# A mixing and low-rank MLP kernel with the order of its first stage rewritten

## The chip, the cores and the metric

One core of a Trainium2 chip runs the whole program. The metric is the device time of one execution in microseconds (us). Five engines work side by side, each with its own queue of instructions that it takes in order: TensorE (PE, matrix products into PSUM), VectorE (DVE), ScalarE (ACT), GpSimd (POOL) and SyncE (SP, which here only issues DMAs). DMAs are issued by SP and by POOL.

## The reference

The input x is 8 x 3136 x 256 in float32. Each batch goes through a two-dimensional Fourier transform of which the real part is kept, then through a low-rank mixing along the sequence, then through a two-layer MLP along the channels, with two residual sums:

```
X = real(fft(fft(x, axis=1), axis=2))      # per batch: sequence, then channels
h = X.transpose(0, 2, 1) @ U @ V           # U: 3136 x 32, V: 32 x 3136
u = X + h.transpose(0, 2, 1)
out = u + maximum(u @ w_ch1, 0) @ w_ch2    # w_ch1: 256 x 1024, w_ch2: 1024 x 256
```

## The kernel before, in words

The sequence transform is a product with tables of sines (tabs, `tabs[0]`) and cosines (tabc, `tabs[1]`), which the kernel computes itself. Symmetries cut it down: a batch of x is loaded forwards (xf) and reversed (xr), in two halves a = 0, 1 of the sequence each; the sums and differences of both, along the sequence and along the channels, are what is multiplied. This is the *fold*: `along_d` (L247 to 251) and `alone` (L253) work along the channels into EOF_ and EOR_, `mirror` (L257) and `half` (L261) along the sequence into G, one G for each parity and for even and odd batches. The tables have eight rows of tiles i = 0 to 7. Rows i = 0, 2, 4, 6 come from `pho` and are called odd rows here, rows 7, 5, 3, 1 come from `phe` and are called even rows: of an even row only half is computed, and `mirror_even` (L234) copies the other half.

The first stage, which builds the tables and the rest, has an order written out by hand (`tc.manual_schedule()` up to `order.close()`): each engine takes its instructions in the order of the source. After it the Tile framework's scheduler orders the instructions itself, and a barrier for the scheduler alone (`tc.no_sync_barrier()`) separates the two. What the stage holds:

- `phase` (L155 to 159), two DVE operations, reduces an angle to a whole number of a turn; `sine` (L161) is one ACT operation, `cosine` (L167) two.
- `cosine_odd(i)` (L240) derives an odd row of the cosine table from the sine table by one ACT copy. `cosine_even` computes an even row from `phe` and mirrors it.
- `halve(t)` (L225, DVE) scales row 7 of table t.
- `fold_u` (L180, DVE, six operations) folds U, which is loaded forwards (UF: two indirect DMAs issued by POOL, L52) and reversed (UR), into GU.
- `transform_u(typ)` (L199) multiplies folded U with table typ and appends the result to the tables, so that the product of x with U comes out of the same matmuls as the transform. It is a generator of four steps: contract on PE with the odd rows (pk = 1), its evict on ACT, contract with the even rows (pk = 0), its evict. `us` and `uc` are its lists of steps for the sine and the cosine table: us[0] and uc[0] need only odd rows, us[2] and uc[2] only even rows.
- MSN, MC: small tables for the transform along the channels, from the phase `pd`.
- POOL clears G of odd batches, VA and TA (L442 to 449), and later issues the loads of the weights (L499 to 504), converts half of W1 (L507), and issues the gathers of xf for the next batch (`load_f`, L52). SP issues the loads of xr (`load_r`, L69) and of one odd row of both (`load_0`, L75 and 78). `load_x(b)` is all of these for a batch.
- Steps 8 and on of `transform(0)`: eight `seq` (L264: eight or four matmuls each into pt, L297; every second one has its result combined by DVE into A, B and tab), eight `chan` (the transform along the channels, L322 to 326, into S and T), `lowrank` (L329: TA, and one row of VA).

Then the main loop runs over 49 chunks of 512 rows: `front(c)` (L355) forms u with the matmul ph (L360) and two DVE sums (L368), `first_product` (L374, relu on ACT at L382), `second_product` (L385, matmuls at L396, sums by DVE at L402 to 405). The steps of `transform(b)` for the next batch, the fold first, are spread over the chunks by a list of due places (`due`).

The hand-written order in the middle of the first stage, before:

```
phases and sines of odd rows; phases, sines and mirrors of even rows
halve(0); fold_u(); POOL: memsets of G[1], VA, TA, iota of pint
cosine_odd x4; us[0]; us[1]; cosine_even(7); cosine_even(5); us[2]; us[3]
cosine_even(3); cosine_even(1); uc[0]
xr halves 0 and 1 along the channels (DVE; odd columns on POOL)
phase of pd; uc[1]; MSN, MC; halve(1); uc[2]; uc[3]
xf along the channels, mirror, half; POOL: weights; load_x(1); seq ...
```

Of the kernel before, what the change touches and what calls it, by code (L numbers as in the profile page):

```python
# [11 lines left out]
FP32 = mybir.dt.float32  # L12
# [7 lines left out]
NI = 8  # L20
NQ = 393
# [6 lines left out]
def kernel(  # L28
# [9 lines left out]
    nc = tc.nc  # L38
# [8 lines left out]
    cpool = ctx.enter_context(tc.tile_pool(name="cpool", bufs=1))  # L47
# [13 lines left out]
    xf = cpool.tile([KP, 2, NI, D], FP32, name="xf")  # L61
    xr = cpool.tile([KP, 2, NI, D], FP32, name="xr")

    def load_f(b, a):
        gather(xf[:PQ, a].rearrange("p i d -> p (i d)"), x, B * S // 8 - 1,
               xidx[:PQ, b, a:a + 1], 8 * D, D)

    def load_r(b, a):
        nc.sync.dma_start(out=xr[:PQ, a].rearrange("p i d -> p (i d)"), in_=rev(x, b, a, D))  # L69

    def load_0(t, dst_f, dst_r, b, w):


        lo = t.offset + b * S * w
        nc.sync.dma_start(out=dst_f[PQ:KP],  # L75
                          in_=bass.AP(t.tensor, lo + (NI - 1) * w,
                                      [[w, 1], [HALF * w, 2], [-w, NI], [1, w]]))
        nc.sync.dma_start(out=dst_r[PQ:KP].rearrange("p a i d -> p a (i d)"),
                          in_=bass.AP(t.tensor, lo, [[w, 1], [HALF * w, 2], [1, NI * w]]))

    def load_x(b):
        for a in range(2):
            load_f(b, a)
            load_r(b, a)
        load_0(x, xf, xr, b, D)

    order = ExitStack()
# [15 lines left out]
                      in_=bass.AP(moe_U.tensor, moe_U.offset + (S - 784) * R,  # L103
                                  [[8 * R, PQ], [-HALF * R, 2], [1, 8 * R]]))
# [17 lines left out]
    EOR_ = cpool.tile([KP, 2, NI, 258], BF16, name="eor")  # L122
# [9 lines left out]
    def const(v):  # L132
# [8 lines left out]
    tabs = [cpool.tile([KP, NI, 2, QW], BF16, name="tabs", tag="tabs"),  # L141
            cpool.tile([KP, NI, 2, QW], BF16, name="tabc", tag="tabc")]
# [18 lines left out]
    def sine(out_, y, bits, sgn):  # L161
        unit = TWO_PI / 2 ** bits
        pp = out_.shape[0]
        nc.scalar.activation(out_, y, AF.Sin, scale=-sgn * unit,
                             bias=(c_pi if sgn > 0 else c_npi)[:pp])

    def cosine(out_, y, bits):  # L167
        pp = y.shape[0]
        ab = gen.tile(list(y.shape), FP32, tag="ab", name="ab")
        nc.scalar.activation(ab[:], y, AF.Abs, bias=c_half[bits][:pp])  # L170
        nc.scalar.activation(out_, ab[:], AF.Sin, scale=TWO_PI / 2 ** bits, bias=c_nhp[:pp])  # L171

    NH = NQ // 2 + 1
    pho = gen.tile([KP, NI // 2, 2, NQ], I32, name="pho", bufs=1)
    phe = gen.tile([KP, NI // 2, 2, NH], I32, name="phe", bufs=1)
# [4 lines left out]
    def fold_u():  # L180
        nc.vector.tensor_tensor(uo[:], UF[:], UR[:, :, ::-1, :], op=AL.subtract)
        nc.vector.tensor_tensor(ue[:], UF[:], UR[:, :, ::-1, :], op=AL.add)
        for par in range(2):
            op = AL.add if par == 0 else AL.subtract
            nc.vector.tensor_tensor(GU[par][:, 0], uo[:, 0], uo[:, 1], op=op)  # L185
            nc.vector.tensor_tensor(GU[par][:, 1], ue[:, 0], ue[:, 1], op=op)
# [10 lines left out]
    def kp(i):  # L197
        return KP if i == NI - 1 else PQ
# [3 lines left out]
    def transform_u(typ):  # L202

        for pk in (1, 0):
            def contract(pk=pk):
                pu = PU[typ, pk] = psum.tile([P, NI, R], FP32, tag="dft", name="pu", bufs=3)
                for io in range(NI):
                    pn = (io + 1) % 2
                    m = kp(io)
                    j0 = NQ - 1 - (4 * 97 + (io + 1) // 2)  # L210
                    ks = ktiles(pk)
                    for n, i in enumerate(ks):
                        w = tabs[typ][:kp(i), i, pn, j0:j0 + 4 * (m - 1) + 1:4]
                        nc.tensor.matmul(pu[:m, io, :], w, GU[pn][:kp(i), typ, i, :],  # L214
                                         start=(n == 0), stop=(n == len(ks) - 1))

            def evict(pk=pk):
                pu = PU[typ, pk]
                nc.scalar.copy(tabs[typ][:PQ, 0:NI - 1, pk, NQ:QW], pu[:PQ, 0:NI - 1, :])
                nc.scalar.activation(tabs[typ][:, NI - 1, pk, NQ:QW], pu[:KP, NI - 1, :],  # L220
                                     AF.Copy, scale=hv[:KP])
            yield contract
            yield evict

    def halve(t):  # L225
        nc.vector.tensor_single_scalar(tabs[t][:, NI - 1, :, :NQ], tabs[t][:, NI - 1, :, :NQ],
                                       hv[:KP], op=AL.mult)
# [6 lines left out]
    def mirror_even(t, i):  # L234

        odd_m = (i + 1) // 2 % 2 == 1
        sgn = 1.0 if odd_m == (t == 0) else -1.0
        nc.scalar.activation(cells(t, i, 0, 1, NH - 1, 1), cells(t, i, NQ - 1, -1, NH - 1, 0),  # L238
                             AF.Copy, scale=sgn)

    def cosine_odd(i):

        nc.scalar.activation(cells(1, i, 1, 1, NQ - 1, 0), cells(0, i, NQ - 2, -1, NQ - 1, 1),
                             AF.Copy, scale=1.0 if i % 4 == 0 else -1.0)

    def along_d(a, src, dst, part):
        lo, hi = src[:, a, :, 1:128], src[:, a, :, 255:128:-1]  # L247
        if part == 0:
            nc.vector.tensor_tensor(dst[:, a, :, 1:128], lo, hi, op=AL.subtract)
        else:  # L250
            nc.vector.tensor_tensor(dst[:, a, :, 129:256], lo, hi, op=AL.add)  # L251

    def alone(a, src, dst):  # L253

        nc.gpsimd.tensor_copy(dst[:, a, :, 128:257:128], src[:, a, :, 0:129:128])  # L255
# [98 lines left out]
    def front(c):  # L354

        u = cp.tile([P, 2, CH], BF16, tag="u", name="u", bufs=2)
        for s in range(2):
            ph = psum.tile([P, CH], FP32, tag="dft", name="ph", bufs=3)
            for b, lo, hi, col in pieces(c):
                nc.tensor.matmul(ph[:, col:col + hi - lo], TA[b % 2][:, s * P:(s + 1) * P],  # L360
                                 VA[b % 2][:, lo:hi], start=True, stop=True)
            for b, lo, hi, col in pieces(c):
                d = ST[b]
                if lo <= HALF:
                    src = (d["S"] if s == 0 else d["T"])[:, lo:hi]
                else:
                    src = (d["T"] if s == 0 else d["S"])[:, S - lo:S - hi:-1]
                nc.vector.tensor_tensor(u[:, s, col:col + hi - lo], ph[:, col:col + hi - lo],  # L368
                                        src, op=AL.add)
        ut = cp.tile([P, 2 * CH // P, P], BF16, tag="ut", name="ut", bufs=3)  # L370
        nc.sync.dma_start_transpose(out=ut[:], in_=u.rearrange("p s r -> p (s r)"))
        CK[c] = dict(u=u, ut=ut)
# [59 lines left out]
    for m, i in enumerate(range(0, NI, 2)):  # L432
        phase(pho[:, m], krow[:KP], ncol[:KP, i:i + 1], 15)
        sine(tabs[0][:, i, :, :NQ], pho[:, m], 15, 1)
    for m, i in enumerate((7, 5, 3, 1)):
        phase(phe[:, m], krow[:KP, :, NH - 1:], ncol[:KP, i:i + 1], 15)
        sine(tabs[0][:, i, :, NH - 1:NQ], phe[:, m], 15, 1)
        mirror_even(0, i)
    halve(0)
    fold_u()  # L440
    for par in range(2):
        nc.gpsimd.memset(G[1][par][:, :, 258:GW].bitcast(I32), 0)  # L442
    for s in range(2):
# [3 lines left out]
        nc.gpsimd.memset(TA[s][R:R + 1, P:P + 1], -1.0)  # L447
    nc.gpsimd.iota(pint[:], pattern=[[0, 1]], base=D, channel_multiplier=-1)
    nc.gpsimd.memset(pint[0:1], P)
    us, uc = list(transform_u(0)), list(transform_u(1))  # L450
    for i in range(0, NI, 2):
        cosine_odd(i)
    us[0]()
    us[1]()

    def cosine_even(m, i):
        cosine(tabs[1][:, i, :, NH - 1:NQ], phe[:, m], 15)
        mirror_even(1, i)

    cosine_even(0, 7)  # L460
    cosine_even(1, 5)
    us[2]()
    us[3]()
    cosine_even(2, 3)
    cosine_even(3, 1)
    uc[0]()
    for a in range(2):
        for part in range(2):
            along_d(a, xr, EOR_, part)
        alone(a, xr, EOR_)  # L470
    nc.vector.memset(lrow[:, 1, 0:1], 128.0)
    nc.vector.tensor_single_scalar(pcol[:], pcol[:], 1.0 / D, op=AL.mult)
    pd = gen.tile([P, 2 * P], I32, name="pd", bufs=1)
    phase(pd[:], lrow.rearrange("p a l -> p (a l)"), pcol[:], 17)
    uc[1]()
    sine(MSN[:, 0:128], pd[:, 0:128], 17, -1)
    sine(MSN[:, 128:256], pd[:, 128:256], 17, 1)
    cosine(MC[:], pd[:], 17)
# [26 lines left out]
    nc.gpsimd.memset(msr[:, :, 0:1], 1.0)  # L505
    nc.gpsimd.memset(msr[:, :, 1:2], -1.0)
    nc.gpsimd.tensor_copy(W1[:, 1, :], w1t[:])  # L507
    load_x(1)
    for step in list(transform(0))[8:]:
        step()  # L510
    order.close()
    tc.no_sync_barrier()
    setup.close()
    cp = ctx.enter_context(tc.tile_pool(name="cp", bufs=2))
    front(0)

    due = {}
    for b in range(1, B):
# [47 lines left out]
```

## Time and profile before

| what | value |
|---|---|
| median of three runs | 503.09 us (502.71 to 503.56) |
| the profiled execution | 503.75 us in all, span 502.0 us |
| busy share of the span | PE 95%, DVE 62%, ACT 56%, POOL 11% |
| first matmul of U (L214) | 17.00 us after the span's start |
| first matmul of batch 0's transform (L297) | 31.06 us |
| first matmul of the first product (L380) | 50.56 us |
| DMA traffic | 67.13 MB, 134 GB/s on average |

The span runs from the first to the last instruction; the rest of an execution lies around it. In the timeline a line gives the start and the length in us, the engine, the source line, the operation, the tile written and those read, the shape, the number of merged instructions, and in brackets the idle time of the engine before it with what ended it. PE is shown busy while matmuls stand in its pipeline, so its share isn't its speed. The spans of POOL are rough.

### The profile page before, as it was taken

The page shows a single profiled execution, that of the slowest core. Times are in us where ns is not written, and L with a number is a line of the kernel's source. Part 1 is how long each engine was busy: PE and PEld are TensorE (multiplying, and loading weights), DVE is VectorE, ACT ScalarE, POOL GpSimd, SP SyncE. Part 2 cuts the span into 40 slices and gives each one's busy share as a digit, 9 for nine tenths or more (in the row PEclk, how much of TensorE's full clock was granted, in tenths as well). Part 3 has the DMA queues.
Part 4 walks back from the last instruction along what each step waited for, and adds up shares of the span by engine and source line. Part 5 has one row for each costly group of instructions (what it writes and reads, how often), then busy time and mean ns, then how long its engine had stood idle before and what let it go on. Part 6 is the DMA issues. An engine that isn't in the chain of part 4 may idle for free.

```text
span 502.0 us, 8180 instructions
## 1 busy us (share of the span) xinstructions
PE 476.3 (95%) x3152; PEld 305.7 (61%) x3152; DVE 312.0 (62%) x693; ACT 281.6 (56%) x537; POOL 56.3 (11%) x79
## 2 busy tenths in 40 slices
PE   0687999999999999999999999999999999999997
PEld 0653566666666666666666666666666666666665
DVE  9985999999989776963474345344343344344243
ACT  4844644665466544655456544655456544755652
POOL 8460212223141100200000000000000000000000
PEclk9999899999999999999999999999999999999999
DMA  6793797889969983333223332333224332333433
GB/s 187 193 200 108 133 254 206 190 232 255 215 183 239 294 208 88 97 92 114 64 63 85 106 84 60 109 80 110 63 64 85 105 85 63 100 89 107 125 85 126
DMA packets 83472, 67.13 MB, mean 134 GB/s; under 512 B 53467, under 2 KB 79905, under 8 KB 80281
## 3 DMA queue, kind: packets, MB, share of 16 engines
q1 hardware_dynamic: 79864, 51.86, 40.3%
q0 software_dynamic: 3568, 14.76, 11.1%
q8 instruction: 24, 0.39, 0.4%
q14 instruction: 16, 0.12, 0.1%
HBM read 29.26 MB, written 25.69 MB: 109 GB/s over the span
## 4 chain that ended last, share of the span: by engine, by line
PE 93%; DVE 4%; ACT 2%; issue 0%; DVEq 0%; ACTq 0%
PE p L396 34%; PE p L380 34%; PE pt L297 14%; PE ph L360 4%; PE pst L322 2%; PE pst L324 2%; PE pu L214 1%; DVE phe L157 1%; PE ptt L334 1%; DVE pho L159 1%; ACT tabc L171 1%; DVE phe L159 0%; DVE pho L157 0%; ACT tabc L238 0%; ACT ab L170 0%; ACT S L326 0%
## 5 line engine op out<-in xcount | busy, mean ns | idle before, releaser
L382 ACT ACTIVATE h<-p 128x512 bf16<-128x512 f32 x392 | 218.4, 597 | 148.7 <-PE p L380 148.4
L380 PE MATMUL p<-u,w 128*128 128x512 bf16 x784 | 210.3, 381 | 2.0 <-DVE u L368 1.7
L396 PE MATMUL p<-w,h 128*128 128x256 bf16 x1568 | 203.5, 273 | 0.0
L396 PEld LDWEIGHTS <-h 128*128 128x128 bf16 x1568 | 153.2, 98 | 59.0 <-DVE o L405 0.3
L380 PEld LDWEIGHTS <-w 128*128 128x128 bf16 x784 | 76.1, 98 | 65.4 <-issue 5.4
L402 DVE TENSOR_TENSOR o<-p,ut 128x4 f32<-128x4 f32 (+1 forms) x100 | 16.3, 163 | 137.6 <-PE p L396 136.5
L297 PE MATMUL pt<-tabc,g 98*128 98x425 bf16 (+1 forms) x256 | 57.5, 350 | 0.0
L297 PEld LDWEIGHTS <-g 98*128 98x128 bf16 (+1 forms) x384 | 38.3, 100 | 31.5 <-issue 4.4
L405 DVE TENSOR_TENSOR o<-p,ut 128x254 f32<-128x254 f32 (+1 forms) x100 | 40.7, 407 | 0.0
L404 DVE TENSOR_TENSOR o<-p,ut 128x254 f32<-128x254 f32 (+1 forms) x100 | 40.6, 406 | 0.0
L301 ACT COPY ev<-pt 128x425 f32<-128x425 f32 x32 | 16.5, 516 | 39.2 <-PE pt L297 30.6
L368 DVE TENSOR_TENSOR u<-ph,S 128x512 bf16<-128x512 f32 (+15 forms) x64 | 35.0, 556 | 0.8 <-PE ph L360 0.8
L368 DVE TENSOR_TENSOR u<-ph,T 128x512 bf16<-128x512 f32 (+15 forms) x64 | 34.9, 556 | 0.3 <-PE ph L360 0.3
L297 PE MATMUL pt<-tabs,g 98*128 98x425 bf16 (+1 forms) x128 | 30.3, 361 | 0.0
L360 PE MATMUL ph<-va,ta 128*128 128x512 bf16 (+18 forms) x128 | 29.8, 333 | 0.5 <-ACT ta L337 0.5
L52 POOL DMA_INDIRECT xf<-in_x_dram,xidx x16 | 21.5, 1344 | 53.6 <-DVE eof L251 25.2
L310 DVE TENSOR_TENSOR B<-pt,ev 128x393 bf16<-128x393 f32 (+1 forms) x16 | 9.3, 584 | 23.8 <-PE pt L297 23.8
L255 POOL CAST eof<-xf 99x16 bf16<-99x16 f32 x16 | 14.0, 877 | 84.6 <-DVE eos L258 52.9
L214 PE MATMUL pu<-gu,tabs 98*98 98x32 bf16 (+1 forms) x64 | 6.0, 251 | 17.0 <-DVE gu L185 17.0
L322 PE MATMUL pst<-A,mc 128*128 128x392 bf16 (+1 forms) x64 | 21.2, 331 | 0.7 <-DVE A L310 0.7
L258 DVE TENSOR_TENSOR eos<-eof,eor 99x1024 bf16<-99x1024 bf16 (+2 forms) x34 | 21.3, 659 | 0.2
L324 PE MATMUL pst<-B,msn 128*128 128x392 bf16 (+1 forms) x64 | 21.1, 330 | 0.0
(86 smaller groups left out, 290.8 us busy)
## 6 DMA issues: line engine op xcount, KB each, us to landing
out_dram<-o SPq DMA_DIRECT2D x48, 512.0 KB
xr<-in_x_dram SPq DMA_DIRECT2D x16, 784.0 KB
ut<-u SPq DMA_TRANSPOSE x49
w<-in_moe_w_ch_dram POOLq DMA_DIRECT2D x1, 512.0 KB
out_dram<-o SPq DMA_DIRECT2D x4, 128.0 KB
va<-in_moe_V_dram POOLq DMA_DIRECT2D x2, 196.0 KB, 6.4
xf<-in_x_dram,xidx POOLq DMA_INDIRECT x16, 8.6
w<-in_moe_w_ch_dram POOLq DMA_DIRECT2D x1, 256.0 KB, 5.8
```

Source lines behind the costliest of these rows:

```text
L52: nc.gpsimd.indirect_dma_start(out_, None, bass.AP(t.tensor, t.offset, [[w, rows], [1, w]]), bass.IndirectOffsetOnAxis(idx, 0), element_of ...
L258: nc.vector.tensor_tensor(EOS[:, a, :, cols], EOF_[:, a, :, cols], EOR_[:, a, ::-1][:, :, cols], op=op)
L297: nc.tensor.matmul(pt[:], g[:kp(i), i, col:col + P], tabs[t][:kp(i), i, par, :], start=(n == 0), stop=(n == len(mm) - 1))
L322: nc.tensor.matmul(pt[:, :hi - lo], MC[:, h * P:(h + 1) * P], d["A"][:, lo:hi], start=True, stop=False)
L324: nc.tensor.matmul(pt[:, :hi - lo], MSN[:, h * P:(h + 1) * P], d["B"][:, lo:hi], start=False, stop=True)
L360: nc.tensor.matmul(ph[:, col:col + hi - lo], TA[b % 2][:, s * P:(s + 1) * P], VA[b % 2][:, lo:hi], start=True, stop=True)
L368: nc.vector.tensor_tensor(u[:, s, col:col + hi - lo], ph[:, col:col + hi - lo], src, op=AL.add)
L380: nc.tensor.matmul(p1[:], W1[:, s, j * P:(j + 1) * P], k["u"][:, s, :], start=(s == 0), stop=(s == 1))
L382: nc.scalar.activation(k["h"][:, j, :], p1[:], AF.Relu)
L396: nc.tensor.matmul(p2[:, t % w, :], h[:, j, rs], W2[:, j, :], start=(j == 0), stop=(j == JT - 1))
L404: nc.vector.tensor_tensor(o[:, ts, 1:P], p2[:, :w, 1:P], ut[:, ts, 1:P], op=AL.add)
L405: nc.vector.tensor_tensor(o[:, ts, P + 1:D], p2[:, :w, P + 1:D], ut[:, tT, P - 1:0:-1], op=AL.add)
```

## The change

The instructions of the first stage are put into another order, one DMA is added, and the end of the hand-written order moves.

- `fold_u` comes directly behind the phases of the odd rows, `cosine_odd` behind their sines, and us[0] and uc[0] follow, ahead of all work on the even rows. The evict of each comes later, among the even rows.
- The memsets of POOL come behind `alone(0, xr, EOR_)`, the odd columns of the first half of xr. On DVE that half comes ahead of `halve(0)`.
- A DMA on SP's queue that reads two values of the second half of xf into a tile `gate`, which nothing reads, stands in front of `load_x(1)`.
- `front(0)` is now the last part of the hand-written order instead of the first part of the scheduled one.

```
         sine(tabs[0][:, i, :, :NQ], pho[:, m], 15, 1)
+    fold_u()
+    for i in range(0, NI, 2):
+        cosine_odd(i)
+    us, uc = list(transform_u(0)), list(transform_u(1))
+    us[0]()
+    uc[0]()
+
+    def cosine_even(m, i):
+        cosine(tabs[1][:, i, :, NH - 1:NQ], phe[:, m], 15)
+        mirror_even(1, i)
+
     for m, i in enumerate((7, 5, 3, 1)):
         phase(phe[:, m], krow[:KP, :, NH - 1:], ncol[:KP, i:i + 1], 15)
         sine(tabs[0][:, i, :, NH - 1:NQ], phe[:, m], 15, 1)
         mirror_even(0, i)
-    halve(0)
-    fold_u()
+    us[1]()
+    cosine_even(0, 7)
+    uc[1]()
+    cosine_even(1, 5)
+    cosine_even(2, 3)
+    for part in range(2):
+        along_d(0, xr, EOR_, part)
+    alone(0, xr, EOR_)
     for par in range(2):
         nc.gpsimd.memset(G[1][par][:, :, 258:GW].bitcast(I32), 0)
...
     nc.gpsimd.memset(pint[0:1], P)
-    us, uc = list(transform_u(0)), list(transform_u(1))
-    for i in range(0, NI, 2):
-        cosine_odd(i)
-    us[0]()
-    us[1]()
...
-    cosine_even(0, 7)
-    cosine_even(1, 5)
+    halve(0)
     us[2]()
     us[3]()
-    cosine_even(2, 3)
     cosine_even(3, 1)
-    uc[0]()
-    for a in range(2):
-        for part in range(2):
-            along_d(a, xr, EOR_, part)
-        alone(a, xr, EOR_)
+    for part in range(2):
+        along_d(1, xr, EOR_, part)
+    alone(1, xr, EOR_)
...
-    uc[1]()
...
+
+    gate = cpool.tile([1, 2], FP32, name="gate")
+    nc.sync.dma_start(out=gate[:], in_=xf[0:1, 1, 0, 0:2])
     load_x(1)
     for step in list(transform(0))[8:]:
         step()
-    order.close()
-    tc.no_sync_barrier()
     setup.close()
     cp = ctx.enter_context(tc.tile_pool(name="cp", bufs=2))
     front(0)
+    order.close()
+    tc.no_sync_barrier()
```

## The prediction

> **What bounds the kernel now.** I read the chain of the page first, then the timeline of the first 70 us, then the landings of the first loads.
>
> ```profile
> PE 93%; DVE 4%; ACT 2%; issue 0%; DVEq 0%; ACTq 0%
> ```
>
> TensorE (PE) carries the chain nearly everywhere: from about 67 us to the end it has no wait worth naming, so no order of the beginning changes what that stretch takes. The change can only move the moment at which this stretch begins. That moment is set in steps, of which the first is the start of batch 0's transform (the pt matmuls of L297). Here is the timeline up to it, merged lines, start and length in us:
>
> ```profile
> 3.66 1.03 POOL L52 DMA_INDIRECT uf<-in_moe_U_dram,xidx  x1 [0.30 <-issue]
> ...
> 7.53 2.92 DVE L157 TENSOR_SCALAR phe<-krow,ncol 99x394 f32<-99x394 f32 x1
> ...
> 7.91 0.97 POOL L442 MEMSET g<- 99x504 int32 x2
> 8.83 1.40 POOL L444 MEMSET va<- 128x1568 int32 x1
> ...
> 10.83 0.41 DVE L157 TENSOR_SCALAR phe<-krow,ncol 99x394 f32<-99x394 f32 x1
> 10.95 0.62 ACT L164 ACTIVATE tabs<-phe,c 99x394 bf16<-99x394 int32 x1 [2.35 <-DVE phe L159]
> 11.01 1.57 POOL L444 MEMSET va<- 128x1568 int32 x1
> 11.27 1.53 DVE L159 TENSOR_SCALAR phe<-phe 99x394 int32<-99x394 int32 x1
> ...
> 14.65 0.69 DVE L181 TENSOR_TENSOR uo<-uf,ur 99x512 f32<-99x512 f32 x1
> ...
> 16.08 3.08 ACT L243 ACTIVATE tabc<-tabs 99x784 bf16<-99x784 bf16 x4
> ...
> 20.02 1.22 DVE L249 TENSOR_TENSOR eor<-xr 99x1016 bf16<-99x1016 f32 x1 [0.48 <-DMA xr<-in_x_dram]
> ...
> 28.09 3.13 PE L214 MATMUL pu<-gu,tabc 98*98 98x32 bf16 x32 [2.14 <-ACT tabc L238]
> ...
> 31.06 1.58 PE L297 MATMUL pt<-tabs,g 98*128 98x425 bf16 x4
> ```
>
> Three things are to be seen. PE's last product of U (uc[2], 28.09) waits for ScalarE (ACT): its last mirrored cosine row ends at 28.04, and the transform starts when this product is through. ACT is late because it lost 2.35, 0.70 and 0.98 us to waits, the first two for VectorE's (DVE's) even-row phases. And DVE was late with those because of GpSimd (POOL): the same L157 takes 0.41 us at 10.83 and 2.92 us at 7.53, ending just behind the first VA memset (10.23); L159 takes 0.37 to 0.43 us elsewhere and 1.53 us beside the second VA memset, ending just behind it. So while POOL's long memsets run, DVE's phases stand still.
>
> The second step is the way from the transform into the main loop:
>
> ```profile
> 48.69 1.22 DVE L249 TENSOR_TENSOR eof<-xf 99x1016 bf16<-99x1016 f32 x1
> 49.82 0.68 DVE L368 TENSOR_TENSOR u<-ph,S 128x512 bf16<-128x512 f32 x1
> ...
> 50.56 2.11 PE L380 MATMUL p<-u,w 128*128 128x512 bf16 x6 [1.66 <-DVE u L368]
> ```
>
> An operation of batch 1's fold sits on DVE in front of the first u, and PE waits 1.66 us for that u.
>
> **The change, part by part.** All sums go against the profiled execution (span 502.0 us, 503.75 us in all).
>
> *U folded early.* fold_u now stands on DVE behind the odd rows' phases, which end at 7.61. It needs both U gathers; the second is issued at 3.66 and lands 7.1 us later, at 10.76. So this is an added wait of 3.1 us, and queued behind it on DVE are all eight even-row phase operations, for which ACT waits. The fold took from 14.74 (the end of L226) to 17.28, 2.54 us; it now ends at 13.3. PE's us[0] and uc[0] (3.06 us each, L214) then run from about 13.1 to 19.2, off the path. ACT meanwhile has the four cosine_odd copies (3.08 us), now from 8.6 to 11.7: they fill ACT's wait for the even rows, and 3.1 us leave the part of its queue that comes behind them.
>
> *Zeros later.* The memsets (block of L442 to L449, 7.91 to 14.03) now follow the first odd copy of xr (L255) on POOL, which waits for the load of xr half 0. The trace's landing records have the last part of that load at 12.95 (the other parts by 9.2). With the copy's 0.26 us the block starts at 13.2 to 13.5. DVE comes to its even-row phases at 13.3. So the collision isn't removed, it moves along with its victim: the block is shifted by 5.3 to 5.6 us, and so are the phases. [...] Bounds: with no collision the first phase is there at 14.1 and ACT, at 1.07 us for a sine and its mirror, ends the loop at 18.5; if DVE got no turn until the whole block is through (19.3), it ends at 24.4. The old collision is the nearest row, with the same block and the same eight operations in the same order, so I take its end of the loop, 16.18, plus 5.4: **21.5**.
>
> *ACT from there.* Three evicts lie ahead of uc[2] on ACT, 0.43 us each (20.14 to 20.57). Four cosines with mirror: 1.75 us each (20.57 to 22.32), the last to its end 1.83. Sum 1.29 + 5.25 + 1.83 = 8.37, so uc[2] can start at 29.85 and no more at 28.09: **+1.75 us**, by the bounds -1.25 (18.5 + 8.37 = 26.85) to +4.7. DVE in the new order: phases to 19.8, first xr half 2.4 us (22.2), halve(0) 0.42 (22.65; us[2] on PE follows to 25.7, its evict is due at 27.5, so this wait costs nothing), second xr half, landed at 20.02, to 25.1, phase of pd and halve(1) to 26.3. Before, that last one ended at 23.42, so the folded x of parity 0, ready at about 28.05 then, comes at 30.9. The transform asks for it at 32.8 (uc[2] and its 3 us). 1.9 us of cover; when ACT is early, as by the lower bound, DVE isn't pushed either (xr half 1 at 20.02 sets it again) and 28.05 stays under 29.85.
>
> *Loads held.* The gate is one DMA on SP's queue that waits for xf half 1 (issued at 6.27, landing 17.1 us later, 23.4). Behind it on SP stand both xr loads of batch 1 (issued at 19.62 and about 22.4 before; now about 24 and 25) and the two one-row loads (31.84, 32.59; these wait for DVE anyway). Before, 15 of the 16 parts of xf half 1 had landed by 19.75, and DVE came to it only at 25.36 (L249), so an earlier landing brings nothing. The other way, xr of batch 1 is read at 53.74 (L249), and xf of batch 1, whose gathers stand behind the weights on POOL, had landed by 44.1 and is read at 48.69. W1, V and W2 now share more of their time with xr: even 3 us later they are in time. Cost 0, cover over 4 us.
>
> *front(0) inside the fixed order.* The fold of batch 1 can no longer slip in ahead of u: 49.82 - 48.69 = **-1.13 us**, and PE's 1.66 us wait shrinks to about 0.5. But that fold operation is not gone, DVE does it later:
>
> ```profile
> 64.85 2.37 DVE L262 TENSOR_TENSOR g<-eos 99x2064 bf16<-99x2064 bf16 x2
> ...
> 67.12 1.61 PE L297 MATMUL pt<-tabc,g 98*128 98x425 bf16 x8
> ```
>
> DVE has 0.31 us idle between 48.69 and here, and the folded parity 0 of batch 1 is ready at 66.05, 1.07 us before PE asks. In the new order DVE's work is the same and starts 1.75 later: 67.5 with the idle time taken up. PE comes at 67.12 + 1.75 - 1.13 = 67.74. So the gain holds, but it is about all that DVE allows here.
>
> **Sum**: 1.75 - 1.13 = +0.6 us on a span of 502.0: 502.6, and 504.4 with the 1.75 around it. The profiled execution lies 0.66 above the median of the runs, 503.09, and I carry the difference over to the median: **503.7 us**.
>
> [...] In the profile the table by windows has the granted clock at 0.80 and 0.50 for 50 to 54 us, and matmuls of 512 columns stand 0.43 us apart at 52 to 54 us against 0.22 later; PE had been busy for only 0.82 us between 47.58 and 50.56. If the smaller gap no longer brings the clock down, PE gains about 1.1 us (ACT's 0.52 us for each relu limits it then), reaches batch 1's transform at 66.6 and waits there for DVE until 67.5: +0.4 in all, 503.5; where the new order on PE puts other work there, 502.6. [...]
>
> **Rivals.**
> 1. The collision is milder, 500.7 to 502.0. If U lands 1.5 us earlier, two phases are through before the memsets; if xr half 0 lands by 9.3, most of the block runs beside fold_u. With no collision: -1.25 - 1.13 = -2.4, 500.7. For it: the two events lie within 0.3 us of one another, and each is set by the last of 16 parts of a load. Against: both loads and their order are the same as before.
> 2. POOL keeps DVE out for the whole block, slower. It is decided at 10.2 and 12.6 of the old trace, where DVE got its turn as soon as a VA memset ended; if the short memsets between follow closely enough, it gets none until 19.3: +4.7 - 1.13 = +3.6, 506.7; with one turn only, about +1.5, 504.6 to 505.2.
> 3. The clock stays up at the front: 502.6 to 503.5, as above.
> 4. The change doesn't do what it says: its held loads free nothing that anybody waits for. That is in my sum already.
>
> **Chances.** Forecast (502.9 to 504.5) 45%, rival 1 25%, rival 2 22%, rival 3 8%. About 0.2%, 1.0 us, is what a measurement of this kernel can tell from no change. Faster than 502.1: nearly all of rival 1 and a little of 3, 24%. Slower than 504.1: rival 2 and a quarter of the forecast, 34%. Between: 42%. The range leaves out the far ends of rivals 1 and 2: 501.0 to 505.7.
>
> **What would show it.** Right: DVE idle from 7.6 to about 10.8; L157 or L159 of 1.5 to 3 us beside the memsets, now at 13 to 18 us; ACT waiting some 5 us between cosine_odd and the end of the even rows; uc[2] at 29 to 31; the first L368 straight behind the VA row (L338). Wrong: even-row phases of 0.4 us each with ACT through them by 18.5, or DVE held until 19; a late load of batch 1 on which DVE waits at 50; another order of PE's work in the main loop with waits that before has not.

## The result and the profile after

Over 20 executions each, the changed kernel takes 504.89 us (median, 502.13 to 506.2) and the kernel before 502.95 us (501.04 to 503.7). The ratio is 1.0038 with a 95% interval of 1.0026 to 1.005: slower by 1.9 us. 503.7 was forecast, in a range of 501.0 to 505.7. The profiled executions are 505.07 us (span 503.3) and 503.75 us (span 502.0), 1.3 us apart; the traces explain that difference, and the scatter of single executions is taken up further down.

The timeline of the changed kernel up to batch 0's transform, start and length in us, answers to the one shown of before:

```profile
8.49 3.08 ACT L243 ACTIVATE tabc<-tabs 99x784 bf16<-99x784 bf16 x4
10.61 0.69 DVE L181 TENSOR_TENSOR uo<-uf,ur 99x512 f32<-99x512 f32 x1 [3.01 <-DMA uf<-in_moe_U_dram,xidx]
...
12.87 0.49 POOL L255 CAST eor<-xr 99x16 bf16<-99x16 f32 x1 [4.92 <-DMA xr<-in_x_dram]
...
13.16 2.89 DVE L157 TENSOR_SCALAR phe<-krow,ncol 99x394 f32<-99x394 f32 x1
13.25 0.98 POOL L459 MEMSET g<- 99x504 int32 x2
14.18 1.40 POOL L461 MEMSET va<- 128x1568 int32 x1
...
16.08 1.95 DVE L159 TENSOR_SCALAR phe<-phe 99x394 int32<-99x394 int32 x1
16.15 1.41 POOL L461 MEMSET va<- 128x1568 int32 x1
...
17.95 0.41 DVE L157 TENSOR_SCALAR phe<-krow,ncol 99x394 f32<-99x394 f32 x1
18.07 0.62 ACT L164 ACTIVATE tabs<-phe,c 99x394 bf16<-99x394 int32 x1 [6.50 <-DVE phe L159]
...
21.96 0.53 ACT L238 ACTIVATE tabs<-tabs 99x392 bf16<-99x392 bf16 x1
...
30.89 3.13 PE L214 MATMUL pu<-gu,tabc 98*98 98x32 bf16 x32 [5.14 <-ACT tabc L238]
...
33.86 1.58 PE L297 MATMUL pt<-tabs,g 98*128 98x425 bf16 x4
```

DVE waits 3.01 us for U, folds it, and comes to its first even-row phase 0.1 us before POOL begins its memsets. Both operations of that one phase then stand still: 2.89 us where L157 takes 0.41 alone, 1.95 us where L159 takes 0.37. ACT, which has done its cosine_odd copies by 11.57, is idle for 6.50 us and ends its loop over the even rows at 22.5. The last product of U starts at 30.89 (28.09 before) and the transform at 33.86 (31.06): 2.8 us later.

The way into the main loop, on PE and DVE:

```profile
50.73 0.69 DVE L368 TENSOR_TENSOR u<-ph,S 128x512 bf16<-128x512 f32 x1
51.33 0.68 DVE L368 TENSOR_TENSOR u<-ph,T 128x512 bf16<-128x512 f32 x1
51.47 0.38 PE L380 MATMUL p<-u,w 128*128 128x512 bf16 x1 [0.96 <-DVE u L368]
51.93 1.21 DVE L249 TENSOR_TENSOR eof<-xf 99x1016 bf16<-99x1016 f32 x1
...
64.22 1.92 PE L396 MATMUL p<-w,h 128*128 128x256 bf16 x16 [0.82 <-DVE o L405]
...
66.49 2.37 DVE L262 TENSOR_TENSOR g<-eos 99x2064 bf16<-99x2064 bf16 x2
...
68.02 1.61 PE L297 MATMUL pt<-tabc,g 98*128 98x425 bf16 x8
```

u now comes straight behind the VA row, and PE starts the first product at 51.47, 0.91 later than before. So of the 2.8 us, 1.13 were won back at the front, and 0.76 in the transform: its matmuls changed from 0.35 us apart to 0.18 at 38.8 us, 4.9 us after its start, and before at 37.6, 6.5 us after its start (2.80 - 0.76 - 1.13 = 0.91). From there on the distance stays. The granted clock no longer falls at the front (1.00 in all windows from 48 to 56 us; 0.80 and 0.50 in 50 to 54 us before), yet PE gets nothing from it: it waits 0.82 us for DVE, which is in the middle of batch 1's fold, and reaches batch 1's transform at 68.02, 0.90 later than before. The chain of work that ended last shows it too: from 52 to 63.5 us it runs through DVE's fold of batch 1 (L249, L251) in the changed kernel, and mostly through PE in the kernel before. DVE's last operation is 0.91 later; the rest of the 1.3 us is in the landing of the last outputs.

### The profile page after: what moved, and what is told of

The parts are those of the page before. It is cut to its first block, busy times and chain, and to the rows that moved or that the text cites. A ratio compares the mean times of both kernels' runs of the same rounds, so it can differ in the third digit from the quotient of the medians.

```text
span 503.3 us, 8125 instructions
## 1 busy us (share of the span) xinstructions
PE 471.4 (94%) x3097; PEld 305.1 (61%) x3152; DVE 311.3 (62%) x693; ACT 281.3 (56%) x537; POOL 52.7 (10%) x79
## 4 chain that ended last, share of the span: by engine, by line
PE 89%; DVE 4%; ACT 3%; DMA 1%; issue 1%; POOL 0%; DVEq 0%; POOLq 0%; ACTq 0%
PE p L396 34%; PE p L380 31%; PE pt L297 14%; PE ph L360 4%; PE pst L322 2%; PE pst L324 2%; DMA uf<-in_moe_U_dram,xidx 1%; PE ptt L334 1%; PE pu L214 1%; DVE phe L157 1%; ACT tabc L171 1%; DVE eor L251 0%; DVE eof L251 0%; DVE eor L249 0%; DVE eof L249 0%
## 5 line engine op out<-in xcount | busy, mean ns | idle before, releaser
L380 PE MATMUL p<-u,w 128*128 128x512 bf16 x735 | 201.7, 379 | 3.3 <-DVE u L368 1.2
L405 DVE TENSOR_TENSOR o<-p,ut 128x254 f32<-128x254 f32 (+1 forms) x100 | 40.9, 409 | 0.0
L360 PE MATMUL ph<-va,ta 128*128 128x512 bf16 (+14 forms) x122 | 28.0, 327 | 0.8 <-ACT ta L337 0.5
L255 POOL CAST eof<-xf 99x16 bf16<-99x16 f32 x16 | 12.3, 776 | 82.9 <-DVE eos L258 53.6
## 6 DMA issues: line engine op xcount, KB each, us to landing
va<-in_moe_V_dram POOLq DMA_DIRECT2D x2, 196.0 KB, 13.5
```

Source lines behind the costliest of these rows:

```text
L380: nc.tensor.matmul(p1[:], W1[:, s, j * P:(j + 1) * P], k["u"][:, s, :], start=(s == 0), stop=(s == 1))
L405: nc.vector.tensor_tensor(o[:, ts, P + 1:D], p2[:, :w, P + 1:D], ut[:, tT, P - 1:0:-1], op=AL.add)
```

## The experiments

Theory A, from the prediction: the even-row phases on DVE stand still for as long as POOL's memsets run, ACT follows, and the start of the transform with it; at the front, what PE wins is given back to DVE's fold of batch 1. The rivals have letters in the expectations, and some letters (C, F) stand for different things in different runs: the wait for U is the loss (B), the clock carries the differences (C in the run with front(0) alone, E), the hold of the loads does something (D), the hold of DVE has another cause than the length of the memsets (G). Each kernel was compared with the kernel before on the same chip; ratios are to that kernel, with 95% intervals. Its own median there was 502.63, 502.69 or 503.32 us, so ratios of different groups of runs compare to about 0.1%.

**Memsets back to the front.**

```
+    (POOL's block of memsets and pint)
     fold_u()
     for i in range(0, NI, 2):
         cosine_odd(i)
...
     alone(0, xr, EOR_)
-    (POOL's block of memsets and pint)
```

> The changed kernel, with POOL's block of memsets moved ahead again, directly behind the two small iotas, so that it runs from about 8 to 14 us, beside DVE's wait for U and the fold of U. Theory A (the collision): DVE's even-row phases now start at 13.2 and take 0.4 us each, ACT is through the even rows at 18.4 instead of 22.5, the last product of U starts at 26.8 instead of 30.9, batch 0's transform at 29.9 instead of 33.9, about 3 to 4 us less in all than the changed kernel, 2 us less than the kernel before. Theory B (the wait for U on DVE is itself the loss): the transform does not start before the 31.06 us of the kernel before, and the time is not below that of the kernel before.

501.15 us, ratio 0.9979 (0.9964 to 0.9995). DVE and ACT of this kernel:

```profile
13.77 0.41 DVE L157 TENSOR_SCALAR phe<-krow,ncol 99x394 f32<-99x394 f32 x1
14.22 0.37 DVE L159 TENSOR_SCALAR phe<-phe 99x394 int32<-99x394 int32 x1
```

```profile
14.62 0.62 ACT L164 ACTIVATE tabs<-phe,c 99x394 bf16<-99x394 int32 x1 [3.05 <-DVE phe L159]
```

The phases take 0.41 and 0.37 us, the last product of U starts at 27.43, the transform at 30.40; that is 0.5 to 0.6 us later than expected, as U was there 0.6 us later in this profile (the fold starts at 11.20). Nothing but the place of the memsets differs from the changed kernel, so 3 us of its time (by the ratios; 3.7 by the medians) are the collision, and theory B fails as the whole cause: the wait for U is still there. But 3.05 us of ACT's idle time remain, and those belong to that wait. The gain on the kernel before, 1.1 us by the ratio, is less than the 2 us expected.

**Memsets later, in the kernel before, and nothing else.**

```
     for a in range(2):
         for part in range(2):
             along_d(a, xr, EOR_, part)
         alone(a, xr, EOR_)
+        if a == 0:
+            (POOL's block of memsets and pint)
```

> The kernel before, with the block of memsets alone moved behind the odd columns of the first half of xr on POOL; U is folded behind the even rows as before. Theory A: the even-row phases run undisturbed from 7.6 to 10.7, U is folded by 13.7, and no operation of DVE that the memsets can hold is left beside them at 13 to 19; ACT could start the last product of U at about 25, so that DVE's fold of x (ready at 28.0) sets the start of the transform: 28 instead of 31.1, and the time 2 to 3 us below the kernel before. Theory B (ACT's and DVE's own work is the limit, not the collision): the start stays within 1 us of 31.1.

500.18 us, ratio 0.9958 (0.9943 to 0.9974). The phases run from 7.52 to 10.7, the transform starts at 27.71 and its first matmul waits 0.20 us for DVE's fold of x (L262), as expected. So the edit that does harm in the changed kernel is worth 2.1 us alone (by the ratio), where front(0) alone, below, is worth nothing that can be measured: with U folded late the phases are through long before the memsets begin. The early fold of U was not run alone. The same rows show two more things about DVE and POOL side by side:

```profile
12.94 2.99 POOL L255 CAST eor<-xr 99x16 bf16<-99x16 f32 x1 [4.83 <-DMA xr<-in_x_dram]
15.84 0.97 POOL L443 MEMSET g<- 99x504 int32 x2
```

POOL's small copy, 0.26 us elsewhere, takes 2.99 us while DVE's two-input sums (fold_u, then L249 and L251 to 15.8) run without a gap; the memsets come only behind it. Beside the memsets it was otherwise: L157 took 2.89 us there in the changed kernel, and the sums of fold_u in the first experiment, beside the memsets that ran up to 12.91 us, took their usual 0.69 and 0.42 us. So which of the two engines stood still differed with the operations on both; why, no run shows. How long the copy is held varies, though: beside the last sums of fold_u it took 0.49 us in the changed kernel and 0.27 in the next run.

**The length of the block.** The changed kernel with the two memsets of VA moved to DVE:

```
-        nc.gpsimd.memset(VA[s][:].bitcast(I32), 0)
...
+    for s in range(2):
+        nc.vector.memset(VA[s][:].bitcast(I32), 0)
     us[1]()
```

> The changed kernel with the two memsets of VA taken from POOL to DVE, behind the even-row phases; G's and TA's stay on POOL where they are. Theory A (DVE's phases stand still for as long as POOL's memsets run): the hold shrinks with the block, from 4.1 us to about 1.3; the first even-row phase is ready at about 15.2 instead of 18.05, ACT is through the even rows at about 19.7 instead of 22.5, and the time falls 2 to 3 us below the changed kernel, to 502 to 503. Rival G (the hold comes from something else than the memsets' length, such as the loads that land in that stretch): the phases stay at 2 to 3 us and the time within 0.7 us of the changed kernel.

501.64 us, ratio 0.9965 (0.9953 to 0.9978), 3 to 4 us below the changed kernel, a little more than expected. The profile is of the longest of its eight executions, 503.28 us.

```profile
13.25 1.54 DVE L157 TENSOR_SCALAR phe<-krow,ncol 99x394 f32<-99x394 f32 x1
14.82 0.60 DVE L159 TENSOR_SCALAR phe<-phe 99x394 int32<-99x394 int32 x1
15.35 0.41 DVE L157 TENSOR_SCALAR phe<-krow,ncol 99x394 f32<-99x394 f32 x1
```

The block is 2.8 us shorter, and the first phase is ready at 15.42 instead of 18.03, 2.6 us sooner, though the loads land as before (the copy in front of the memsets starts at 13.17). ACT is through the even rows at 19.9, and the transform starts at 31.69 instead of 33.86. The hold is set by the length of POOL's memsets; rival G falls. This is the same order as the changed kernel's in all else, and it beats the kernel before.

**No gate.**

```
-    gate = cpool.tile([1, 2], FP32, name="gate")
-    nc.sync.dma_start(out=gate[:], in_=xf[0:1, 1, 0, 0:2])
     load_x(1)
```

> The changed kernel without the DMA that holds back the loads of batch 1. Theory A: nobody waits for what the hold brings; xr of batch 1 is issued from about 21.3 us, the start of the transform stays within 0.3 us of 33.9 and the time within 0.5 us of the changed kernel. Rival D (the hold works): the second half of xf lands at 23.4 instead of 22.4 and something behind it on POOL or DVE is late, 0.5 to 1 us more than the changed kernel.

504.02 us, ratio 1.0028 (1.0005 to 1.005), which overlaps the changed kernel's. The transform starts at 33.30, 0.56 earlier than in the changed kernel, more than expected; but the cause stands before the gate could act: the memsets fell differently between the phases (2.54, 0.37, 1.65, 0.43 us for the first four operations instead of 2.89, 1.95, 0.41, 0.37):

```profile
13.58 2.54 DVE L157 TENSOR_SCALAR phe<-krow,ncol 99x394 f32<-99x394 f32 x1
...
16.43 1.65 DVE L157 TENSOR_SCALAR phe<-krow,ncol 99x394 f32<-99x394 f32 x1
16.55 0.62 ACT L164 ACTIVATE tabs<-phe,c 99x394 bf16<-99x394 int32 x1 [4.97 <-DVE phe L159]
...
18.58 0.63 ACT L164 ACTIVATE tabs<-phe,c 99x394 bf16<-99x394 int32 x1 [0.84 <-DVE phe L159]
```

The last part of the second half of xf landed at 22.4 with the gate and without it, and DVE takes that half at 28.09 or 27.86. No effect of the gate is shown in either direction; by the two intervals an effect of up to 1 us is not excluded.

**The front alone.** The kernel before with front(0) in the fixed order:

```
-    order.close()
-    tc.no_sync_barrier()
     setup.close()
     cp = ctx.enter_context(tc.tile_pool(name="cp", bufs=2))
     front(0)
+    order.close()
+    tc.no_sync_barrier()
```

> The kernel before, with front(0) alone taken into the hand-written order. Theory A: the first L368 comes straight behind the VA row, PE's first L380 about 1.1 us earlier; the clock may stay up there, but DVE has folded batch 1 no sooner, so that PE reaches batch 1's transform at 66.0 to 67.1 instead of 67.1: between 0 and 1.1 us less than the kernel before. Rival C (the clock carries it): 1.1 us and the slow 3.4 us stretch both count in full, 2 us or more less.

502.33 us, ratio 1.0 (0.9987 to 1.0014): no gain that can be measured. In its profile the first product starts at 49.42 instead of 50.56, the clock stays up (1.0 in the mean), and batch 1's transform starts at 65.97, 1.15 earlier. There, just behind DVE's fold, it stops paying:

```profile
64.45 2.37 DVE L262 TENSOR_TENSOR g<-eos 99x2064 bf16<-99x2064 bf16 x2
```

Parity 0 is folded at 65.6, 0.3 us ahead of PE. That the 1.15 us of this execution don't show in the medians has a part of its answer in the mean clocks of the single executions. The profile of before, in which the clock fell at the front, has a mean of 0.996. Of the 35 executions of the kernel before that were measured beside this one, 17 have 0.995 or 0.996, and they took 502.5 to 503.8 us; the other 18 have 0.999 or 1.0, and 14 of them took 501.1 to 501.5. The 12 of this kernel all have 0.999 or 1.0 and took 501.2 to 501.6 (four) or 502.3 to 502.6 (eight). So the two profiles compare an execution with the fall to one without it, and against the executions of before without it the edit gains nothing. Why is open.

**Front and an early start of batch 1's fold.** front(0) and front(1) in the fixed order, and three operations of the fold in DVE's idle time:

```
+    steps0, steps1 = list(transform(0))[8:], list(transform(1))
+    for step in steps0[:-1]:
+        step()
+    steps1[0]()
+    alone(0, xr, EOR_)
+    along_d(0, xr, EOR_, 0)
+    steps0[-1]()
...
     front(0)
+    front(1)
```

> The kernel before, with front(0) and front(1) in the hand-written order and the first three DVE operations of batch 1's fold put into DVE's idle time ahead of the VA row. Theory A (DVE's fold of batch 1 holds back what PE wins at the front): the folded batch 1 is ready about 3 us sooner than with front(0) alone (61 to 63 us for parity 0 instead of 65.6), PE reaches batch 1's transform at about 64 to 65 instead of 65.97, and the time falls by 1 to 2 us against front(0) alone. Rival C (DVE isn't the limit there): PE reaches it at 66 as before and the time stays.

501.07 us, ratio 0.998 (0.9966 to 0.9994). The folded batch 1 is ready at 61.3, as expected, and its transform starts at 61.80, sooner than the 64 to 65 expected. The medians, 1.3 us apart, go the way of theory A: with the fold out of the way the front pays. It is not shown beyond doubt, as the intervals of the two ratios overlap, front(1) moved with the rest, and some of the difference between the two profiles is the clock, which came up 4.3 us after the transform's start here and 6.5 us after it with front(0) alone.

**All three together** (memsets later, both fronts, early fold, in the kernel before):

> The kernel before with three edits together: the block of memsets behind the first odd copy of xr, front(0) and front(1) in the hand-written order, the start of batch 1's fold in DVE's idle time. U is folded late and nothing is held. Theory A: the gains add, about 2.4 for the memsets and 1 to 2 for the front: 498 to 499.5 us, less than any kernel so far. Rival C: no better than the memsets alone (500.2).

500.33 us, ratio 0.9966 (0.995 to 0.9983). The gains do not add; the expectation was wrong. The profile names two parts of it: the early fold pushes the VA row to 44.90, u to 45.93, and PE waits 1.26 us there; and the clock falls at the front again (0.50 from 48 to 50 us, 0.997 in the mean of the execution), so that the first 20 matmuls of the first product take 6.37 us, where they take 5.02 without the memsets' edit. The row, which chunk 3 is the first to read, was moved behind both fronts:

```
+        if b:
+            last_row(b)
...
     front(1)
+    last_row(0)
```

> Memsets later, front(0) and front(1) in the fixed order and the early start of batch 1's fold, as in the combination, with one more edit: the row of VA (0.96 us on DVE, first read by chunk 3) comes behind both fronts. In the combination this row stood between the early fold and u, and u came 1.3 us behind PE's ph. Theory A: u follows ph at once, PE's first L380 is 0.5 to 1 us earlier, 499.5 to 500 us. Rival C: the front is off the path, no change from 500.3.

500.56 us, where the kernel before took 503.32 in the runs beside it: ratio 0.9949 (0.9928 to 0.9969). PE's first wait falls to 0.73 us and its first product starts at 46.15 instead of 46.90, as expected; the median does not reach the 499.5 to 500 expected, and the interval overlaps that of the three together. And with matmuls that keep PE busy at the front:

```
     steps0[-1]()
+    keep_busy(3)
...
     front(0)
+    keep_busy(6)
     front(1)
```

> As the one before, with 3 matmuls behind the low-rank product and 6 behind the ph of chunk 0 whose results nothing reads, to keep PE busy between the transform of batch 0 and the first product. Theory E (short idle stretches at the front bring the clock down in some executions): the clock stays up there in the profile, and the slower executions go, 0 to 1 us less in the median. Rival F: the matmuls only stand in PE's way, 0.3 to 1 us more.

500.43 us, ratio 0.9945 (0.9931 to 0.996), six executions between 500.28 and 500.68. The clock stays up in the profile (1.0 in the mean), as it also does without the extra matmuls, whose seven executions lay between 498.87 and 501.94: the longer ones are gone, the shorter ones too, and the median is the same. The combinations and the memsets alone can't be ranked by their intervals; all beat the kernel before and the changed one.

**PE kept busy early.** This run goes back to the three edits together, and adds 20 matmuls whose results nothing reads ahead of the first product of U and 8 ahead of the last:

```
+    keep_busy(20)
     us[0]()
     us[1]()
...
     uc[0]()
+    keep_busy(8)
```

> As the one before, with idle stretches of PE filled by matmuls whose results nothing reads: 20 ahead of the first product of U, 8 ahead of the last. Theory E (the spread of the times and the slow half of batch 0's transform come from the clock): the matmuls of the transform stand 0.18 us apart from the start instead of 0.35, the transform ends 1.5 to 3 us sooner (DVE's fold of the second half of the columns allows no more), and the times of the executions lie closer together: 496 to 498.5 us. Rival F: the small products of U between let the clock fall again; then no gain.

500.78 us, ratio 0.9971 (0.9951 to 0.999): no gain, as rival F had it, though not quite for its reason: the clock had fallen before the small products began, and they did not bring it up. The table by windows has the granted clock in the column before the DMA share:

```profile
6.00:10.00 4.00, 4.00 (x15) 1.86 (x13) 3.86 (x10) 3.34 (x6) 2.16 (x5) 1.00 0.98 298
13.00:16.00 3.00, 0.44 (x6) 0.44 (x6) 3.00 (x8) 2.97 (x5) 2.19 (x8) 0.51 1.00 229
20.00:24.00 4.00, 4.00 (x46) 4.00 (x45) 3.90 (x10) 3.87 (x9) 3.69 (x8) 0.50 0.90 292
28.00:32.00 4.00, 4.00 (x29) 2.78 (x29) 3.90 (x6) 1.17 (x4) 0.42 (x3) 0.50 1.23 182
34.00:38.00 4.00, 4.00 (x24) 2.16 (x23) 1.45 (x4) 0.51 (x1) 1.11 (x2) 1.00 0.79 204
```

The clock came up at 9.7 us, 4.8 us into the 20 matmuls of 393 columns, it fell at 13.1 in the gap that follows (PE idle from 10.7 to 15.6), and from 15.6 to 24 us PE is busy without a gap on products of 32 columns, and the clock stays at 0.50, also through the 8 large matmuls (24.3 to 27.1). It came up again at 33.6, 3.7 us after the first matmul of 425 columns. This profile also had the first half of xr landed at 9.5 us instead of 12.4 in the three together, so that the memsets caught the last even-row phase after all (L157 at 9.87: 2.63 us).

## Why the prediction was right, and where it was not

*The sign and the mechanism held.* The even-row phases on DVE met POOL's memsets at their new place, and ACT and the last product of U came late by it; the first two experiments and the one on the length of the block show that this is the cause. DVE was to be idle from 7.6 to 10.8, and was, to 10.61. U was to be folded at 13.3, and was, at 13.24. The memsets were to start at 13.2 to 13.5, and did, at 13.25. ACT's way from the last even row to the last product was to take 8.37 us and took 8.34 (22.50, where the first evict could start, to 30.84). u was to follow the VA row and gain 1.13 us, and did, to the hundredth. DVE's fold of batch 1 was to allow PE hardly more than that, and PE waited for it (0.82 us at 64.22, L405 behind the fold). The condition of rival 3 came true as well, the clock stayed up (1.00 from 48 to 56 us); it brought nothing, as DVE set the pace. What keeps it up or brings it down there, no run shows.

*The step that was mis-sized is the end of ACT's loop.* It was put at 21.5, the old collision moved by 5.4 us; the measured end of the last even row is 22.5. DVE's phases lost 4.1 us here and 3.7 before, nearly the same. What differs is where: before, the first VA memset caught the first phase and the second VA memset the second phase, while ACT was busy with the first row; here both caught the two operations of the first phase, and ACT had nothing. The start of uc[2] came 2.8 us later and not 1.75. That is rival 2's milder case, "with one turn only, about +1.5, 504.6 to 505.2", at 22%, and the median, 504.89, lies there and above the forecast's own 502.9 to 504.5. In the run without the gate the two holds fell on different phases again, and ACT had its first two even rows at 16.55 and 18.58, close to the old rows moved by 5.4 us (16.35 and 18.23). So in these three profiles the price depends on which operation stands in front when a memset ends, and the forecast took one fall of it as the rule.

*The size in all.* Of the 1.94 us between the medians 0.62 were forecast. The mis-sized step adds 1.05, the transform takes away 0.76, the landing of the last outputs adds 0.41, and the two profiled executions lie differently to their medians, 0.80 us above it before and 0.18 after, which adds 0.62. The forecast had none of the last three. The 0.76 us came from a clock that rose 1.6 us sooner after the transform's start, and that the first product came 0.91 us late, not far from the forecast's 0.6, is luck by that.

*The scatter.* Of the 20 executions of the changed kernel three took under 503 us, the rest 504.5 to 506.2; the kernel before has a group at 501.0 to 501.4 and another at 502.6 to 503.7. The fall of the clock at the front goes with the groups of the kernel before, as the mean clocks above show, but not with those of the changed kernel: all 20 have 0.999 or 1.0. Two other causes are left, and neither is shown. One is the loads: by the traces' landing records the first half of xr landed at 9.2 to 10.5 us in three of the profiles, at 11.5 to 13.3 in the others, each time for the sake of the last one or two of its landings. That a load which lands early moves the memsets to another place is shown by the profile with PE kept busy; that it makes the groups of times is not, since the changed kernel was not profiled in such an execution. The other is the moment at which the clock rises in batch 0's transform, 3.7 to 6.5 us after its start in the profiles, with matmuls 0.35 us apart until then and 0.18 after. That "both loads and their order are the same as before" was used against rival 1; the order is, the landings are not.

*The held loads* were costed at nothing, and no run contradicts that.

## What to carry to other kernels

Ask of every moved block on POOL what DVE does at its new place: here the same memsets cost 3 us beside tensor_scalar phases and left two-input sums at their usual length (0.69 us), and one of the edits alone was worth 2.1 us where all of them together lost 1.9. Two edits that both depart from one collision can meet again at the next; the time at which each is released, not the order in which they are written, decides. And where two engines are near their limit, a gain at one of them is worth only what the other's slack allows (here PE won 1.13 us at the front and then waited 0.82 us for DVE), so look for the second before taking the first.

## What the runs showed of the hardware

The clock was not raised by small products: 8 us of PE without a gap on matmuls of 32 columns (16 to 24 us, with PE kept busy early) left it at 0.50, while it rose after 4.8 us of matmuls of 393 columns, and after 3.7 to 6.5 us of matmuls of 425 columns in batch 0's transform. What sets the moment within that spread, no run shows. At the front the clock fell in the profile of before at 51.22 us, 13.65 us behind its rise, and for 3.41 us. PE was not idle all the time ahead of the fall: in the last 3.41 us before it PE was busy for 1.48 us there, for 1.54 with the memsets later alone and for 1.64 with the three edits together. In the changed kernel it was busy for 1.72 us of the 3.41 us that lie as far behind the rise of its clock (49.05 to 52.46), and the clock stayed up. Whether that difference decides was not shown.

The column of the granted clock reads 1.00 until the first change that a trace records: at 34 to 36 us of before, too, where matmuls of 425 columns stood 0.35 us apart instead of 0.18. Later in that trace matmuls of 512 columns stood 0.43 us apart where the column reads 0.50 (52 to 54 us) and 0.22 where it reads 1.00, so at the start of these traces the spacing of the matmuls tells more of the clock than the column.

POOL's copy waited for the last part of its load: in the changed kernel 13 of the 15 recorded landings of the first half of xr came by 10.0 us and the last two at 12.67 and 12.74, and the copy started at 12.87, with the memsets behind it.
